# P^T of the second and third token group: 32x32 block transposes on VectorE and a way through DRAM in place of TensorE transposes

## The chip, the cores and the metric

The kernel runs on one core of one Trainium2 chip. The core has five engines that run side by side and wait for each other by semaphores: PE (TensorE, the matrix engine; PEld is its loading of weights), DVE (VectorE), ACT (ScalarE), POOL (GpSimd) and SP (SyncE, which here issues DMA transfers). The time is that of one execution in microseconds, the median of several runs; less is better.

## The reference, cut to what matters

Attention over a sliding window of 64 keys, and on its output a dense mixture of four experts with weights from `domain_probs`. The sizes are B = 4, H = 8, S = 576, D = 64; N = 2304 tokens, DM = 512, E = 4, F = 1024.

```python
scores = (1 / sqrt(D)) * (q @ k.T)                 # per batch and head
rel = pos[:, None] - pos[None, :]
scores = where((rel >= 0) & (rel < 64), scores, -1e9)
attn = exp(scores - scores.max(-1)); attn = attn / (attn.sum(-1) + 1e-9)
x = (attn @ v)  as (N, H * D)                      # P V
p = domain_probs / (domain_probs.sum(-1) + 1e-9)
for e in range(4):
    out += p[:, e] * (relu(x @ w1[e]) @ w2[e])
```

## The kernel before, in words

The 2304 tokens are cut into three token groups of 768 (`NGRP`, index n), and the attention into 36 groups of 64 queries (index g, twelve per token group: g 0 to 11, 12 to 23, 24 to 35). For one attention group, four pairs of heads are worked on together, so a tile has 128 partitions (two heads of 64 queries) and 4 x 128 columns (four pairs, 128 keys; only 64 keys where a batch begins). The steps of a group, with the names that the planner gives them, are:

- S (L302): scores on PE into a PSUM bank `sb`.
- m (L332, L336): DVE scales, masks and takes the row maximum; e (L343): ACT takes the exponentials, in `sm`; r (L352, L353): DVE takes the reciprocals of the sums; n (L360): POOL multiplies, which gives the normalised P in `sm`.
- T (L367): PE transposes P, four times 128 x 128, into a PSUM bank `tb`; t (L374): ACT or DVE copies it to `pt` in SBUF.
- V (L388): for two groups at a time, PE multiplies P^T with the values `vn` into `vb`; x (L398): ACT or DVE copies the result into `xr`, which is x transposed, for the token group.

The expert layer takes one unit of 256 hidden features at a time, 16 units per token group, 48 in all (index i). Seven products of a Strassen-like scheme, P1 to P7 (L623, 384 columns, six matmuls each, float32r as two parts "high" and "low"), give the hidden values of unit i in the banks X, Y and V; G steps (L707, y, 512 columns) multiply them with w2. The first two units of the first token group are done directly (d, L676). Between the products DVE forms sums from the banks (u2, u3, c22, c21, c12, all L642); the product P7 may only start when u2 has been read out of bank Y, P4 when u3 has, P3 when c22 has. ACT and DVE then make the two parts of the hidden values (hh L549, hl L552), which the G steps wait for. The weights come by DMA into `w1r` and `w2r`; POOL forms four combinations of w1 (L485), and ACT and DVE split them (L498, L502). When a token group is full, its quarters are combined and split by L423, L428 and L438 (tiles B and T).

The order is not written out by hand. A `Planner` holds every step with a cost per engine, a due time, the steps that it follows and the buffers that it takes; `order()` deals them out to the engines, and each engine then runs its instructions strictly in that order. PE's products and G steps have a fixed sequence among themselves (`seq`); the attention of the next token group is put between them. SP's transfers are steps too, and a transfer that waits for a buffer holds up those behind it on SP.

The change touches `Step.__init__` (L32), `admit` (L58) and the cost of SP steps (L105) in the planner, the list of buffers (L156), `make` (L192), and the steps T, t and V of a group (L364 to L393).

Of the kernel before, what the change touches and what calls it, by code (L numbers as in the profile page):

```python
# [8 lines left out]
F32 = mybir.dt.float32  # L9
# [11 lines left out]
LATENCY = dict(PE=0.25, ACT=0.12, DVE=0.12, POOL=0.15, SP=1.0)  # L21
# [9 lines left out]
class Step:  # L31
    def __init__(self, plan, name, engines, emit, due, after=(), takes=(), uses=(), seq=None, port=()):  # L32
        self.name, self.engines, self.emit, self.due, self.seq, self.port = name, engines, emit, due, seq, port
        self.after, self.takes, self.uses = [a for a in after if a is not None], list(takes), list(uses)
        self.done = None
        self.next = []
        for b in {*self.takes, *self.uses}:
            b.left += 1
        self.waits = len(self.after)
        for a in self.after:  # L40
            a.next.append(self)
        plan.steps.append(self)


class Planner:
# [5 lines left out]
    def order(self):  # L51
        clock = dict.fromkeys(("PE", "ACT", "DVE", "POOL", "SP"), 0.0)
# [3 lines left out]
        out = []  # L56

        def admit(s):  # L58
            slack = 0.6 if "PE" in s.engines and s.seq is None else 0.0
            s.ready = max((a.done + LATENCY[a.engine] for a in s.after), default=-slack) + slack  # L60
            for e in s.engines:
                ready[e].append(s)

# [4 lines left out]
        while left:  # L68
# [22 lines left out]
            t, e, s = best  # L91
# [11 lines left out]
            if e in s.port:  # L103
                port_free = end
            if e == "SP":  # L105
                clock[e] = t + 0.5
                dma_free = end = max(dma_free, t + 1.5) + s.engines[e]
            s.start, s.done, s.engine = t, end, e
            if s.seq is not None:
# [19 lines left out]
def kernel(ctx: ExitStack, tc: tile.TileContext, q, k, v, dprobs, w1, w2, out):  # L129
    nc = tc.nc  # L130
# [22 lines left out]

    slots = {}
    for kind, n in dict(
        qb=3, kt=2, vn=4, sm=3, pt=3, st=4, xr=1, w1r=2, w1a=1, w1b=1, w1c=1, w1d=1, w2r=1, w2s=3, h0=6, h1=8,  # L156
        s1=1, u2=1, u3=1, c22=1, c21=1, c12=1, acc=TPB * 2, B11=1, B21=1, B22=1, T1=1, T2=1, T3=1, T4=1,
    ).items():
        slots[kind] = [f"{kind}_{i}" for i in range(n)]
# [17 lines left out]
    dps = pool.tile([P, N // P, 1], F32, tag="dps", name="dps")  # L177

    SHAPES = dict(
        qb=([P, NP, P], F32), kt=([P, NP, W + P], F32), vn=([P, DM], F32), sm=([P, NP, P], F32), pt=([P, NP, P], F32), st=([P, 4, NP], F32),  # L180
        xr=([P, KC, G], F32), w1r=([P, 7, A], F32), w1a=([P, 2, 2, A], F32R), w1b=([P, 2, 2, A], F32R),
        w1c=([P, 2, 2, A], F32R), w1d=([P, 2, 1, A], F32R), w2r=([P, 2, DM], F32), w2s=([P, 2, 2, DM], F32R),
        h0=([P, 2, T], F32R), h1=([P, 2, T], F32R), acc=([P, DM], F32),
# [28 lines left out]
    def add(name, engines, emit, due, after=(), takes=(), uses=(), seq=None, port=()):  # L212
        return Step(plan, name, engines, emit, due, after, takes, uses, seq, port)
# [43 lines left out]
    for g in range(NG):  # L257
# [7 lines left out]
        nk = nkeys(g)  # L265
        u, o = divmod(g, 2)
        qb, vn, sm, pt, st = Buf("qb" + z), Buf("vn" + z), Buf("sm"), Buf("pt"), Buf("st")
        sb, tb = Buf("pa" + z), Buf("pa" + z)
        both = n > 0 or j >= GPB
        if j % 2 == 0 or not both:  # L270
            vb, pairs = Buf("pa" + z), []
# [92 lines left out]
        def transp(on, g=g, nk=nk, sm=sm, tb=tb):  # L364
            t = make(tb, f"tb{g}")
            for p in range(NP):
                nc.tensor.transpose(t[:nk, p * P : (p + 1) * P], sm.tile[:, p, :nk], ident)  # L367

        tr = add(f"T{g}", dict(PE=0.45), transp, due + 3, [nm], [tb], [sm])
        t_step[g] = tr  # L370

        def evac_t(on, g=g, nk=nk, tb=tb, pt=pt):
            t = make(pt, f"pt{g}").rearrange("s p j -> s (p j)")
            (nc.vector.tensor_copy if on == "DVE" else nc.scalar.copy)(t[:nk], tb.tile[:nk])  # L374

        ev = add(f"t{g}", dict(ACT=0.6, DVE=0.69), evac_t, due + 3.2, [tr], [pt], [tb])

        pairs.append((g, nk, vn, pt, ev, v_dma))
        if j % 2 == 0 and both:
            continue  # L380

        def pv(on, pairs=pairs, vb=vb):
            t = make(vb, f"vb{pairs[0][0]}").rearrange("s (p j) -> s p j", p=NP)
            for x, (_, nk, vn, pt, _, _) in enumerate(pairs):
                for p in range(NP):
                    for i in range(2):
# [446 lines left out]
```

## Time and profile before

| | us |
|---|---|
| median of 3 runs | 843.77 |
| lowest and highest run | 843.57, 844.07 |
| the profiled execution in all | 844.59 |
| span of the profile | 842.8 |
| PE busy | 834.9 (99%) |
| DVE busy | 549.9 (65%) |
| ACT busy | 357.3 (42%) |
| POOL busy | 324.1 (38%) |

The span runs from the first to the last instruction of the program; the execution has a little around it. Busy time of PE overlaps from one matmul to the next, since matmuls are pipelined: what a step costs in PE's queue is seen from the start of one group of matmuls to the start of the next. The granted TensorE clock is full in every slice of the page. In 40 equal slices PE stands at 8 or 9 tenths after the first, and DVE is fullest in the first slices and around 290 us. DMA engines are busy for more than half of a slice only in the first three.

### The profile page before, as it was taken

The page shows a single profiled execution, that of the slowest core. Times are in us where ns is not written, and L with a number is a line of the kernel's source. Part 1 is how long each engine was busy: PE and PEld are TensorE (multiplying, and loading weights), DVE is VectorE, ACT ScalarE, POOL GpSimd, SP SyncE. Part 2 cuts the span into 40 slices and gives each one's busy share as a digit, 9 for nine tenths or more (in the row PEclk, how much of TensorE's full clock was granted, in tenths as well). Part 3 has the DMA queues.
Part 4 walks back from the last instruction along what each step waited for, and adds up shares of the span by engine and source line. Part 5 has one row for each costly group of instructions (what it writes and reads, how often), then busy time and mean ns, then how long its engine had stood idle before and what let it go on. Part 6 is the DMA issues. An engine that isn't in the chain of part 4 may idle for free.

```text
span 842.8 us, 12925 instructions
## 1 busy us (share of the span) xinstructions
PE 834.9 (99%) x4814; PEld 749.5 (89%) x4814; DVE 549.9 (65%) x962; ACT 357.3 (42%) x819; POOL 324.1 (38%) x334
## 2 busy tenths in 40 slices
PE   8999999999999999999999999999999999999998
PEld 7998988888998888898998888889898889889887
DVE  5878755566665896466665766589556556566553
ACT  5756433344444363344443544335334333333320
POOL 4733633424334154443334433326334434434400
PEclk9999999999999999999999999999999999999999
DMA  9953212233233143232333202113312212112102
GB/s 334 288 163 119 90 55 100 75 94 113 81 114 101 63 145 117 84 107 63 121 98 107 88 26 91 61 50 111 115 51 79 71 51 90 61 51 97 31 24 75
DMA packets 45471, 81.23 MB, mean 96 GB/s; under 512 B 6368, under 2 KB 15840, under 8 KB 45408
## 3 DMA queue, kind: packets, MB, share of 16 engines
q1 hardware_dynamic: 44880, 80.14, 28.8%
q8 instruction: 38, 0.62, 0.3%
q10 hardware_dynamic: 528, 0.26, 0.1%
q14 instruction: 25, 0.20, 0.1%
HBM read 75.67 MB, written 4.72 MB: 95 GB/s over the span
## 4 chain that ended last, share of the span: by engine, by line
PE 98%; DVE 1%; DMA 1%; issue 0%; POOL 0%; ACT 0%; DVEq 0%; POOLq 0%
PE y L707 47%; PE Y L623 17%; PE V L623 11%; PE X L623 11%; PE sb L302 4%; PE vb L388 2%; PE d L676 2%; PE tb L367 2%; DMA kt<-in_k_dram 1%; PE yl L576 0%; PE sb L300 0%; DVE sm L332 0%; POOL sm L360 0%; DVE B L428 0%; DVE st L336 0%
## 5 line engine op out<-in xcount | busy, mean ns | idle before, releaser
L707 PE MATMUL y<-w2s,h 128*128 128x512 f32 x1716 | 444.0, 395 | 0.0
L707 PEld LDWEIGHTS y<-w2s,h 128*128 128x128 f32 x1716 | 316.6, 188 | 51.6
L485 POOL TENSOR_TENSOR w1r<-w1r 128x256 f32<-128x256 f32 x184 | 149.7, 819 | 192.7 <-DMA w1r<-in_moe_w_dram 141.0
L524 POOL TENSOR_TENSOR w2s<-w2r,w2s 128x512 fp32r<-128x512 f32 x96 | 132.2, 1389 | 227.6 <-ACT w2s L518 227.5
L642 DVE TENSOR_TENSOR u<-Y,s 128x384 f32<-128x384 f32 x92 | 51.1, 556 | 140.5 <-PE Y L623 140.5
L726 DVE SCALAR_TENSOR_TENSOR acc<-y,dp,acc 128x512 f32<-128x512 f32 x125 | 93.3, 747 | 23.4 <-PE y L707 23.4
L552 DVE SCALAR_TENSOR_TENSOR h<-c,h 128x384 fp32r<-128x384 f32 x138 | 83.6, 609 | 13.5 <-ACT h L549 13.2
L498 ACT CAST w1b<-w1r 128x512 fp32r<-128x512 f32 x46 | 28.5, 620 | 138.8 <-PE Y L623 138.3
L549 ACT ACTIVATE h<-c 128x384 fp32r<-128x384 f32 x138 | 72.3, 525 | 21.2 <-DVE c L642 20.3
L360 POOL TENSOR_TENSOR sm<-sm,st 128x512 f32<-128x512 f32 (+1 forms) x36 | 37.4, 1039 | 78.3 <-DVE st L353 55.7
L518 ACT CAST w2s<-w2r 128x1024 fp32r<-128x1024 f32 x48 | 50.4, 1051 | 25.3 <-PE y L707 21.6
L498 ACT CAST w1a<-w1r 128x512 fp32r<-128x512 f32 x48 | 29.8, 621 | 72.1 <-PE Y L623 68.0
L623 PE MATMUL Y<-T,w1c 128*128 128x384 f32 x276 | 55.8, 337 | 0.8 <-DVE u L642 0.8
L623 PE MATMUL V<-B,w1d 128*128 128x384 f32 x276 | 56.6, 340 | 0.0
L623 PE MATMUL Y<-T,w1b 128*128 128x384 f32 x276 | 56.6, 339 | 0.0
L623 PE MATMUL Y<-T,w1a 128*128 128x384 f32 x276 | 55.9, 337 | 0.0
L623 PE MATMUL X<-B,w1c 128*128 128x384 f32 x276 | 55.8, 336 | 0.0
L623 PE MATMUL X<-B,w1a 128*128 128x384 f32 x276 | 55.7, 336 | 0.0
L623 PE MATMUL V<-T,w1b 128*128 128x384 f32 x276 | 55.5, 335 | 0.0
L343 ACT ACTIVATE sm<-sm,st 128x128 f32<-128x128 f32 (+1 forms) x120 | 46.1, 386 | 21.7 <-DVE st L336 21.0
L623 PEld LDWEIGHTS Y<-T,w1c 128*128 128x128 f32 x276 | 49.3, 188 | 5.4 <-DVE u L642 1.5
L642 DVE TENSOR_TENSOR c<-Y,s 128x384 f32<-128x384 f32 x46 | 25.6, 557 | 43.1 <-PE Y L623 43.1
(79 smaller groups left out, 1016.9 us busy)
## 6 DMA issues: line engine op xcount, KB each, us to landing
w1r<-in_moe_w_dram SPq DMA_DIRECT2D x96, 256.0 KB, 3.5
w2r<-in_moe_w_dram SPq DMA_DIRECT2D x48, 512.0 KB, 3.5
qb<-in_q_dram SPq DMA_DIRECT2D x36, 256.0 KB, 3.8
vn<-in_v_dram SPq DMA_DIRECT2D x32, 256.0 KB, 4.1
kt<-in_k_dram SPq DMA_DIRECT2D x17, 384.0 KB, 5.0
out_dram<-acc SPq DMA_DIRECT2D x17, 256.0 KB, 2.0
vn<-in_v_dram SPq DMA_DIRECT2D x4, 128.0 KB, 4.1
kt<-in_k_dram ACTq DMA_DIRECT2D x1, 256.0 KB, 4.9
```

The costliest lines, as they stand in the source:

```text
L343: nc.scalar.activation(t[:, p, :nk], t[:, p, :nk], AF.Exp, bias=st.tile[:, 1, p : p + 1], accum_out=st.tile[:, 2, p : p + 1],)
L360: nc.gpsimd.tensor_tensor(out=t, in0=t, in1=rl.to_broadcast([P, NP, nk]), op=ALU.mult)
L485: nc.gpsimd.tensor_tensor(out=t[:, dst], in0=t[:, x], in1=t[:, y], op=op)
L498: f(t[:, 0], raw.tile[:, lo_:hi_])
L518: nc.scalar.copy(make(b, f"w2s{i}")[:, 0], raw.tile)
L524: nc.gpsimd.tensor_tensor(out=b.tile[:, 1, f], in0=raw.tile[:, f], in1=b.tile[:, 0, f].bitcast(F32), op=ALU.subtract)
L549: nc.scalar.activation(make(b, f"h{i}_{f}{t_}")[:, 0], src.tile[:, :T], AF.Relu)
L552: nc.vector.scalar_tensor_tensor(out=b.tile[:, 1], in0=src.tile[:, :T], scalar=0.0, in1=b.tile[:, 0].bitcast(F32), op0=ALU.max, op1=ALU.su ...
L623: nc.tensor.matmul(t[:, :T], wb.tile[:, a, wi, ws], cb.tile[:, x, c, :], start=first and m == 0, stop=m == 5, skip_group_check=True,)
L642: return lambda t, p_: nc.vector.tensor_tensor(out=t, in0=p_, in1=o.tile, op=ALU.add)
L707: nc.tensor.matmul(o, hh[:, a, ts], w[:, b, f, :], start=x == 0 and m == 0, stop=x == 1 and m == 5)
L726: nc.vector.scalar_tensor_tensor(out=ab.tile, in0=yb.tile, scalar=pc, in1=ab.tile, op0=ALU.mult, op1=ALU.add)
```

## The change

For the first token group (n = 0) all stays as it was. For the other two, P is no longer transposed on PE. DVE transposes it in blocks of 32 x 32 from `sm` into a tile `tp` (one buffer): in it each block stands where its 32 queries were, and inside it queries and keys are exchanged. SP then stores `tp` by four transfers, one for each 32 partitions, into a DRAM tile `hop` (two buffers), such that the blocks come to lie in the order of the keys, and one load brings `hop` into `pt`. The PSUM bank `tb` and its evacuation fall away for these groups. `pt` now holds, for each key, the four blocks of 32 queries outside and the head pairs inside, so P V reads a head's 64 queries as two runs of 32 columns.

In the planner, a step of P V gets 6 us of slack after its inputs in place of 0.6, the four stores count as four issues, and an issue of SP counts 0.45 in place of 0.5. One buffer of `vn` is given up for `tp`. Numbers below in names are the planner's buffers or running numbers.

```diff
@@ planner
-        self.done = None
+        self.done, self.issues, self.slack = None, 1, 0.6 if "PE" in engines and seq is None else 0.0
...
-            slack = 0.6 if "PE" in s.engines and s.seq is None else 0.0
-            s.ready = max((a.done + LATENCY[a.engine] for a in s.after), default=-slack) + slack
+            s.ready = max((a.done + LATENCY[a.engine] for a in s.after), default=-s.slack) + s.slack
...
-                clock[e] = t + 0.5
+                clock[e] = t + 0.45 * s.issues
@@ buffers
-        qb=3, kt=2, vn=4, sm=3, pt=3, st=4, xr=1, w1r=2, ...
+        qb=3, kt=2, vn=3, sm=3, tp=1, pt=3, hop=2, st=4, xr=1, w1r=2, ...
...
+            b.tile = dram.tile([4, 32, 4, P], F32, tag=b.slot, name=name)
@@ attention group
-        sb, tb = Buf("pa" + z), Buf("pa" + z)
+        sb, tb = Buf("pa" + z), Buf("tp" if n else "pa0")
...
+        else:
+            def transp(on, g=g, nk=nk, sm=sm, tb=tb):
+                t = make(tb, f"tp{g}")
+                blocks = sm.tile[:, :, :nk].rearrange("s p (b j) -> s b p j", j=32)
+                nc.vector.transpose(out=t[:, : nk // 32], in_=blocks)
+
+            t_step[g] = tr = add(f"T{g}", dict(DVE=0.69), transp, due + 3, [nm], [tb], [sm], port=("DVE",))
+
+            hop = Buf("hop")
+
+            def leave(on, g=g, nk=nk, tb=tb, hop=hop):
+                t = make(hop, f"hop{g}")
+                for a in range(4):
+                    nc.sync.dma_start(
+                        t[: nk // 32, :, a].rearrange("b j x -> j b x"),
+                        tb.tile[32 * a : 32 * (a + 1), : nk // 32].rearrange("j b p i -> j b (p i)"),
+                    )
+
+            def place(on, g=g, nk=nk, hop=hop, pt=pt):
+                nc.sync.dma_start(
+                    make(pt, f"pt{g}")[:nk].rearrange("k p j -> k (p j)"),
+                    hop.tile[: nk // 32].rearrange("b j a x -> (b j) (a x)"),
+                )
+
+            ev = add(f"t{g}", dict(SP=2.0), leave, due + 3.2, [tr], [hop], [tb])
+            ev.issues = 4
+            ev = add(f"u{g}", dict(SP=1.5), place, due + 3.4, [ev], [pt], [hop])
...
+                        if n == 0:
+                            pt_head = pt.tile[:nk, p, lo:hi]
+                        else:
+                            pt_head = pt.tile.rearrange("k p j -> k (p j)").rearrange("k (a p i) -> k a p i", a=4, p=NP)
+                            pt_head = pt_head[:nk, 2 * i : 2 * i + 2, p]
...
+        if n:
+            vv.slack = 6.0
```

**Place 1, P V of groups 32 and 33 on PE, and the transfers on SP.** Before, PE transposes group 33 (`tb`) and multiplies the pair (`vb`) two expert products later:

```order
L623 MATMUL V_5280<-B_1_3213,w1d_5237 128x384 x6
L367 MATMUL tb_5384<-ident,sm_5325 128x128 x4
L623 MATMUL X_5393<-B_1_3063,w1a_5273 128x384 x6
L707 MATMUL y_3_5409<-w2s_4942,h_01_5068 128x512 x3
L707 MATMUL y_3_5409<-w2s_4942,h_11_5017 128x512 x3
L388 MATMUL vb_5419<-pt_5227,vn_4759 64x64 x8
L388 MATMUL vb_5419<-pt_5400,vn_4761 64x64 x8
```

Now the pair stands behind the last y step (y_5) of the same two units, where before it stood within y_3:

```order
L662 MATMUL Y_5125<-T_1_3335,w1c_5076 128x384 x6
L746 MATMUL y_5_5203<-w2s_4880,h_01_4948 128x512 x3
L746 MATMUL y_5_5203<-w2s_4880,h_11_4870 128x512 x3
L424 MATMUL vb_5245<-pt_4964,vn_4582 64x64 x8
L424 MATMUL vb_5245<-pt_5143,vn_4928 64x64 x8
L662 MATMUL V_5145<-B_1_3289,w1d_5104 128x384 x6
```

Between the product in front of the old transpose and the new place of P V lie thirteen expert products, seven P and six G. On SP the four stores of group 33 (`hop`, printed as one row) and the load into `pt` now stand among the weight loads; a w1 load is between them:

```order
L552 DMA w2r_5034<-in_moe_w_dram 128x1024
L394 DMA hop_5099<-tp_5089 32x4x128 x4
L514 DMA w1r_5121<-in_moe_w_dram 128x512
L515 DMA w1r_5121<-in_moe_w_dram 128x512
L400 DMA pt_5143<-hop_5099 128x512
```

SP had only loads of weights, q, k and v and the stores of the result before; the row of `pt` is one that waits for transfers in front of it.

**Place 2, the start on PE.** This is unit 2, the first that is done by the seven products: Y is the bank of P6, P7 and P4, then V that of P3. Before:

```order
L623 MATMUL Y_1042<-T_0_913,w1a_892 128x384 x6
L302 MATMUL sb_1051<-kt_745,qb_738 128x128 x4
L623 MATMUL Y_1042<-T_0_883,w1b_932 128x384 x6
L367 MATMUL tb_1077<-ident,sm_990 128x128 x4
L302 MATMUL sb_1087<-kt_745,qb_847 128x128 x4
L623 MATMUL Y_1042<-T_0_935,w1c_904 128x384 x6
L623 MATMUL V_982<-B_0_819,w1d_687 128x384 x6
```

Now:

```order
L662 MATMUL Y_1010<-T_0_908,w1a_883 128x384 x6
L304 MATMUL sb_1020<-kt_749,qb_742 128x128 x4
L662 MATMUL Y_1010<-T_0_886,w1b_927 128x384 x6
L662 MATMUL Y_1010<-T_0_966,w1c_905 128x384 x6
L662 MATMUL V_957<-B_0_826,w1d_689 128x384 x6
```

The transpose of group 14 is gone, and the scores of group 17 have moved behind, so P7, P4 and P3 follow each other directly. On DVE the second u of this unit now stands ahead of two weight splits (w1a, w1b), behind which the sum c comes; before, both splits stood ahead of that u.

**Place 3, DVE at the end of unit 15**, where the third token group takes over. The y product that is second in PE's queue for the next unit pair waits for `h_10`. Before:

```order
L642 TENSOR_TENSOR c_15_3188<-Y_3108,s_15_3068 128x384
L726 SCALAR_TENSOR_TENSOR acc_5_1209<-y_5_3146,dp,acc_5_1209 128x512
L642 TENSOR_TENSOR c_15_3204<-V_3071,u_15_3125 128x384
L332 SCALAR_TENSOR_TENSOR sm_3216<-sb_3127,mask 128x512
L336 TENSOR_REDUCE st_3215<-sm_3216 128x4
L502 TENSOR_TENSOR w1c_3176<-w1r_2907,w1c_3176 128x512
L552 SCALAR_TENSOR_TENSOR h_11_3179<-c_15_3168,h_11_3179 128x384
L502 TENSOR_TENSOR w1d_3199<-w1r_2907,w1d_3199 128x256
L552 SCALAR_TENSOR_TENSOR h_10_3201<-c_15_3188,h_10_3201 128x384
```

Now, from the row after that first c (`c_15_3245`) on:

```order
L541 TENSOR_TENSOR w1b_3192<-w1r_2936,w1b_3192 128x512
L541 TENSOR_TENSOR w1c_3242<-w1r_2936,w1c_3242 128x512
L591 SCALAR_TENSOR_TENSOR h_11_3240<-c_15_3227,h_11_3240 128x384
L765 SCALAR_TENSOR_TENSOR acc_5_1182<-y_5_3185,dp,acc_5_1182 128x512
L467 TENSOR_TENSOR T_1_3215<-xr_1191,T_1_3215 128x768
L681 TENSOR_TENSOR c_15_3291<-V_3113,u_15_3173 128x384
L334 SCALAR_TENSOR_TENSOR sm_3297<-sb_3207,mask 128x512
L338 TENSOR_REDUCE st_3296<-sm_3297 128x4
L334 SCALAR_TENSOR_TENSOR sm_3315<-sb_3284,mask 128x4x64
L338 TENSOR_REDUCE st_3314<-sm_3315 128x4
L541 TENSOR_TENSOR w1d_3276<-w1r_2936,w1d_3276 128x256
L591 SCALAR_TENSOR_TENSOR h_10_3279<-c_15_3245,h_10_3279 128x384
```

Two pairs of score reductions stand ahead of `h_10` in place of one (the second of 64 keys), and w1b and a split of T have come into this stretch. On PE two score steps (25 and 26) have moved from just ahead of that y product to a place before the product whose sum is this first c, and the score step of 27 stands where they were.

## Rows read from the trace of the kernel before

**Rows 1.** the page, busy time of each engine: us (share of the span) xinstructions

```profile
PE 834.9 (99%) x4814; PEld 749.5 (89%) x4814; DVE 549.9 (65%) x962; ACT 357.3 (42%) x819; POOL 324.1 (38%) x334
```

**Rows 2.** timeline of PE, 136 us: start us, us, engine, line, operation, operands

```profile
135.92 0.60 PE L367 MATMUL tb<-ident,sm 128*128 128x128 f32 x4
136.28 1.32 PE L623 MATMUL X<-B,w1c 128*128 128x384 f32 x6
137.43 1.56 PE L707 MATMUL y<-w2s,h 128*128 128x512 f32 x6
138.83 1.20 PE L623 MATMUL Y<-T,w1c 128*128 128x384 f32 x6
139.87 1.55 PE L707 MATMUL y<-w2s,h 128*128 128x512 f32 x6
```

**Rows 3.** stretch, length, busy of PE, PEld, DVE, ACT, POOL; clock, DMA, GB/s

```profile
90.00:282.00 192.00, 192.00 (x1125) 172.47 (x1125) 122.34 (x209) 81.86 (x178) 76.39 (x79) 1.00 0.28 90
282.00:314.00 32.00, 32.00 (x169) 28.39 (x168) 30.88 (x48) 17.52 (x46) 11.66 (x12) 1.00 0.37 120
```

**Rows 4.** timeline of PE near 78 us

```profile
77.11 0.60 PE L367 MATMUL tb<-ident,sm 128*128 128x128 f32 x4
77.54 1.06 PE L302 MATMUL sb<-kt,qb 128*128 128x128 f32 x8
79.44 1.32 PE L623 MATMUL Y<-T,w1c 128*128 128x384 f32 x6 [0.84 <-DVE u L642]
```

**Rows 5.** groups by line, DVE: busy us, mean ns, idle before, releaser

```profile
L374 DVE COPY pt<-tb 128x512 f32<-128x512 f32 (+1 forms) x10 | 6.8, 684 | 1.3 <-PE tb L367 1.3
...
L423 DVE CAST T<-xr 128x768 fp32r<-128x768 f32 x3 | 1.7, 556 | 0.2
```

**Rows 6.** timeline of DVE near 78 us

```profile
78.23 0.68 DVE L502 TENSOR_TENSOR w1b<-w1r,w1b 128x512 fp32r<-128x512 f32 x1
78.83 0.55 DVE L642 TENSOR_TENSOR u<-Y,s 128x384 f32<-128x384 f32 x1
```

**Rows 7.** timeline of DVE near 300 us

```profile
295.96 1.79 DVE L502 TENSOR_TENSOR w1b<-w1r,w1b 128x512 fp32r<-128x512 f32 x1
297.67 0.54 DVE L642 TENSOR_TENSOR c<-Y,s 128x384 f32<-128x384 f32 x1
...
299.26 0.67 DVE L332 SCALAR_TENSOR_TENSOR sm<-sb,mask 128x512 f32<-128x512 f32 x1
...
300.57 1.23 DVE L502 TENSOR_TENSOR w1c<-w1r,w1c 128x512 fp32r<-128x512 f32 x1
...
302.52 1.01 DVE L552 SCALAR_TENSOR_TENSOR h<-c,h 128x384 fp32r<-128x384 f32 x2
```

**Rows 8.** timeline of PE near 300 us

```profile
295.52 1.55 PE L707 MATMUL y<-w2s,h 128*128 128x512 f32 x6
...
301.42 1.95 PE L302 MATMUL sb<-kt,qb 128*128 128x128 f32 x16
303.13 1.63 PE L707 MATMUL y<-w2s,h 128*128 128x512 f32 x6
```

**Rows 9.** DMA issues: count, KB each, median us from issue to landing

```profile
qb<-in_q_dram SPq DMA_DIRECT2D x36, 256.0 KB, 3.8
...
kt<-in_k_dram SPq DMA_DIRECT2D x17, 384.0 KB, 5.0
out_dram<-acc SPq DMA_DIRECT2D x17, 256.0 KB, 2.0
```

**Rows 10.** timeline of SP, the issue of a w1 load

```profile
195.01 0.33 SPq L475 DMA_DIRECT2D w1r<-in_moe_w_dram  x1
```

**Rows 11.** timeline of POOL, its first combinations of that load

```profile
200.37 1.89 POOL L485 TENSOR_TENSOR w1r<-w1r 128x256 f32<-128x256 f32 x2 [0.81 <-DMA w1r<-in_moe_w_dram]
```

**Rows 12.** timeline of ACT, the split of w1a from them

```profile
215.94 0.62 ACT L498 CAST w1a<-w1r 128x512 fp32r<-128x512 f32 x1 [2.03 <-PE Y L623]
```

**Rows 13.** timeline of PE, P V of a pair

```profile
489.79 1.15 PE L388 MATMUL vb<-pt,vn 128*64 128x64 f32 x32
```

More of the change, by code (lines that the diff above doesn't have):

```diff
@@ L155 @@
     for kind, n in dict(
-        qb=3, kt=2, vn=4, sm=3, pt=3, st=4, xr=1, w1r=2, w1a=1, w1b=1, w1c=1, w1d=1, w2r=1, w2s=3, h0=6, h1=8,
+        qb=3, kt=2, vn=3, sm=3, tp=1, pt=3, hop=2, st=4, xr=1, w1r=2, w1a=1, w1b=1, w1c=1, w1d=1, w2r=1, w2s=3, h0=6, h1=8,
         s1=1, u2=1, u3=1, c22=1, c21=1, c12=1, acc=TPB * 2, B11=1, B21=1, B22=1, T1=1, T2=1, T3=1, T4=1,
@@ L168 @@
     pool = ctx.enter_context(tc.tile_pool(name="pool", bufs=1))
+    dram = ctx.enter_context(tc.tile_pool(name="dram", bufs=1, space=bass.MemoryType.DRAM))
     psum = ctx.enter_context(tc.tile_pool(name="psum", bufs=1, space=bass.MemoryType.PSUM))
@@ L179 @@
     SHAPES = dict(
-        qb=([P, NP, P], F32), kt=([P, NP, W + P], F32), vn=([P, DM], F32), sm=([P, NP, P], F32), pt=([P, NP, P], F32), st=([P, 4, NP], F32),
+        qb=([P, NP, P], F32), kt=([P, NP, W + P], F32), vn=([P, DM], F32), sm=([P, NP, P], F32), pt=([P, NP, P], F32), tp=([P, 4, NP, 32], F32), st=([P, 4, NP], F32),
         xr=([P, KC, G], F32), w1r=([P, 7, A], F32), w1a=([P, 2, 2, A], F32R), w1b=([P, 2, 2, A], F32R),
@@ L194, in make @@
             b.tile = psum.tile([P, DM], F32, tag=b.slot, name=name)
+        elif b.kind == "hop":
+            b.tile = dram.tile([4, 32, 4, P], F32, tag=b.slot, name=name)
         else:
@@ L362 @@
         nm = add(f"n{g}", dict(POOL=0.05 + 0.00203 * NP * nk), norm, due + 2, [r], [], [sm, st], port=("POOL",))
[L364 to L374, printed above, removed]
@@ L376, with evac_t, transp @@
-        ev = add(f"t{g}", dict(ACT=0.6, DVE=0.69), evac_t, due + 3.2, [tr], [pt], [tb])
+        if n == 0:
+            def transp(on, g=g, nk=nk, sm=sm, tb=tb):
+                t = make(tb, f"tb{g}")
+                for p in range(NP):
+                    nc.tensor.transpose(t[:nk, p * P : (p + 1) * P], sm.tile[:, p, :nk], ident)
+            tr = add(f"T{g}", dict(PE=0.45), transp, due + 3, [nm], [tb], [sm])
+            t_step[g] = tr
+            def evac_t(on, g=g, nk=nk, tb=tb, pt=pt):
+                t = make(pt, f"pt{g}").rearrange("s p j -> s (p j)")
+                (nc.vector.tensor_copy if on == "DVE" else nc.scalar.copy)(t[:nk], tb.tile[:nk])
+            ev = add(f"t{g}", dict(ACT=0.6, DVE=0.69), evac_t, due + 3.2, [tr], [pt], [tb])
+        else:
+            def transp(on, g=g, nk=nk, sm=sm, tb=tb):
+                t = make(tb, f"tp{g}")
[18 more added lines that the diff above has]
+            ev = add(f"u{g}", dict(SP=1.5), place, due + 3.4, [ev], [pt], [hop])
@@ L380, with pv @@
             continue
-        def pv(on, pairs=pairs, vb=vb):
+        def pv(on, pairs=pairs, vb=vb, n=n):
             t = make(vb, f"vb{pairs[0][0]}").rearrange("s (p j) -> s p j", p=NP)
@@ L387, in pv @@
                         lo, hi = i * D, (i + 1) * D
+                        if n == 0:
+                            pt_head = pt.tile[:nk, p, lo:hi]
+                        else:
+                            pt_head = pt.tile.rearrange("k p j -> k (p j)").rearrange("k (a p i) -> k a p i", a=4, p=NP)
+                            pt_head = pt_head[:nk, 2 * i : 2 * i + 2, p]
                         nc.tensor.matmul(
                             t[lo:hi, p, x * W : (x + 1) * W], vn.tile[:nk, p * P + lo : p * P + hi],
-                            pt.tile[:nk, p, lo:hi], start=True, stop=True,
+                            pt_head, start=True, stop=True,
                         )
         vv = add(f"V{g}", dict(PE=0.2 + 0.47 * len(pairs)), pv, due + 4, [y for z_ in pairs for y in z_[4:]], [vb], [y for z_ in pairs for y in z_[2:4]])
+        if n:
+            vv.slack = 6.0
         def evac_x(on, n=n, lo=(j + 1 - len(pairs)) * W, hi=(j + 1) * W, vb=vb):
```

## The prediction

> **What bounds the kernel now.** I read the table of engines first. TensorE (PE) is busy for 834.9 of 842.8 us, VectorE (DVE) for 549.9, ScalarE (ACT) for 357.3, GpSimd (POOL) for 324.1 [rows 1]. The chain of waits says the same from the end backwards: PE's lines fill nearly all of it. The timeline of PE, third, shows the products of the expert layer start to start without a pause [rows 2]. So a microsecond taken from PE's queue is a microsecond of the kernel, unless PE then waits; one added elsewhere is free until PE waits for it. Where that could happen is read from the stretches, fourth: between 90 and 282 us DVE is busy 122.3 of 192.0 us, but 30.9 of 32.0 us between 282 and 314, where the second token group takes over [rows 3]. The other place where PE waits for DVE is at the start, 0.84 us at 79.44 [rows 4]. The change adds DVE work at both.
>
> **What leaves PE.** 24 steps of four transposes (groups 12 to 35) leave. Bars overlap, so I count starts. The transposes start at 135.92 and the next product at 136.28: 0.36 us. That product, the first after float32 work, takes until 137.43, 1.15 us, where the same kind takes 1.04 (138.83 to 139.87) [rows 2]. So a step costs 0.36 + 0.11 = 0.47 us among products. The three that touch another float32 step (12, 13, 14) cost 0.43 (77.11 to 77.54 [rows 4]). 21 x 0.47 + 3 x 0.43 = 11.2; since the starts are rounded to 0.01 us, I take **-11.0 us**. Their evacuations go too, nearly all from ACT, which was waiting for PE anyway: nothing for the sum.
>
> **What DVE gets.** 24 block transposes of 128 x 512. The trace has none. The cheapest pass over SBUF is a cast of 768 columns in 0.56 us, so 0.37 for 512; two passes of the evacuation's length would be 1.37. I take 0.69, the copy of just these elements, the nearest row [rows 5]. 24 x 0.69 = 16.6 us, against 69.7 idle us in the second stretch alone [rows 3], where it is hidden by DVE's waiting for PE. Each transpose waits for POOL's normalisation and holds up what is behind it on DVE; its place comes when that is due, as PE's did.
>
> The Trainium skill ("VectorE: DVE Perf Modes", sections The three transpose paths and Rules for kernel authors) speaks against such a move: TensorE for a 128x128 transpose where a PSUM destination is fine; its table gives VectorE 311 ns for one in bf16 and TensorE 390. As an estimate from that table a step would be 4 x 0.311 = 1.24 us on DVE, near the upper end above and so near the first rival below; its 390 ns is not what PE pays here, where four take 0.36 us.
>
> **The transition at 300 us.** The order puts two score reductions (the pairs of L332 and L336, in the changed file L334 and L338) ahead of the split h_10 that the second y product waits for. Before, DVE ran without a gap from the sum c at 297.67 to the two splits that start at 302.52, the first of which, 0.55 long, is the one: 5.40 us [rows 7]. Now the stretch has in addition w1b (0.60 start to start [rows 6]), a split of T of 768 columns (half as much again, 0.90) and a half-width reduction, an estimate of 0.9 between the half and the whole of the full pair's 1.31 (299.26 to 300.57): 7.8 us. PE covers it from the end of the product before c (295.52) to the y product (303.13): 7.61 us, of which two score steps take 1.71 [rows 8]. These two now stand earlier and one of 0.9 comes in: cover 6.8. So PE waits **+1.0 us**. Bounds: 0, if DVE starts c early, and 2.1, if w1b meets POOL again as in the 1.79 us that it took at 295.96 [rows 7].
>
> **The start.** In before P4 waits for u at 79.44, with transposes and a score step ahead of it since 77.11 [rows 4], and u at 78.83 stands behind two weight splits [rows 6]. Now transposes and score step leave that place and u goes ahead of the splits: it ends near 78.2, P4 starts at 78.25, and the next sum c behind the two splits lets P3 start near 79.9. Before, P3 started 1.15 after P4, at 80.6. That is 0.7 us earlier, with 0.43 + 0.9 us of PE work gone from between: 0.65 is not gained, **+0.7**. The first 60 us are dealt anew too, since loads and buffers differ. Between 0, where all goes as before, and twice the 0.84 that PE waits here, I take **+0.5**, for the shorter queue in which transposes and P V cover each other.
>
> **The way through DRAM.** For each group SP issues four stores of 64 KB and a load of 256 KB, and the load waits in SP's queue until the stores have landed. Stores land 2.0 us after issue, q loads of 256 KB 3.8, kt's 5.0 [rows 9]; an issue takes 0.33 [rows 10]. So 0.69 + 4 x 0.33 + 2.0 + 0.33 + 3.8 = 8.1 us from transpose to P^T; with 5.0 for both landings, issues twice as long and 1.37 for the transpose 14.7. P V stands later by enough: of pair 32/33, six y products of 1.40 and seven of 1.04 [rows 2] lie between the place of the old transpose and the new one of P V, 15.7 us. So PE does not wait: **0**. Behind the waiting load stand w1, w2, q, k and v loads, late by 2 to 4 us. A w1 load issued at 195.01 [rows 10] is first used by POOL at 200.37, two of its four combinations take 1.89 us [rows 11], and the cast of w1a at 215.94 waited not for them but for PE to leave the old buffer [rows 12]: 15.6 - 3.8 = 11.8 us are spare. One vn buffer less moves v loads, whose data P V now needs later.
>
> **P V itself** keeps its matmuls, but reads P^T as two runs of 32 columns instead of one of 64. A pair takes 1.15 us [rows 13]. The trace has no float32 operand in split runs. Bounds: 0 and, if split runs stream at half speed, 12 x 1.15 = 13.8 us. I take 0: its own row, with the same count of columns, is the nearest. Below nothing it can't go, for the columns stay.
>
> **Sum.** -11.0 + 1.0 + 0.7 + 0.5 = -8.8 us. The profiled execution took 844.59 us in all, so 835.8; the runs' median, 843.77, is 0.8 below it. I predict **835.0 us**.
>
> **Rivals.**
> *DVE becomes a bound at the pinch points.* If a transpose costs 1.37 us, each of those in the full stretches (three before 90 us, one near 290) adds 0.7, and w1b's long form another 1.1: 835.0 + 3.9 = 838.9. For it: DVE is 96% busy there [rows 3]. Against: most transposes fall where DVE waits for PE.
> *SP's queue turns the gain round (slower).* The load waits for four stores of 512-byte pieces, and everything behind it on SP waits too. Up to a hop of 15.7 us nothing is lost; beyond that each of 12 pairs loses the excess. From 16.5 us on (12 x 0.8 = 9.6) the kernel is slower than before; at 17 it loses 12 x 1.3 = 15.6, so 835.0 + 15.6 = 850.6. For it: SP works strictly in order, and stores of that shape are not in the trace. Against: twice the landing time of a store still fits.
> *Two runs of 32 stream slowly:* 835.0 + 13.8 = 848.8. It turns the sign from 8.8 / 12 = 0.73 us a pair.
> *Nothing waits:* 843.8 - 11.0 = 832.8, if PE's waits for DVE do not grow at all.
>
> **How the numbers follow.** The forecast (833.5 to 837) has 0.72; nothing waits 0.08; the DVE pinch 0.11; SP's queue 0.05; slow runs 0.04. A change under 0.2% (1.7 us) can't be told from none. Faster: 0.72 + 0.08 + 0.10 = 0.90; slower 0.07, the last two less their mild forms; same 0.03, those and the worst of the pinch. The range 832.3 to 840.0 holds the first three cases and leaves the last two out.
>
> **What would show it.** Right: no transposes on PE after 50 us and P V pairs still 1.15 us long; the block transpose near 0.69; a wait of PE for DVE of about 1 us at the second y product after the change of token group, and two smaller ones near 76 to 80 us; no wait of P V for the load of pt; SP waiting about 2 us before each such load. Wrong: P V waits for a DMA, P V's bar grows, or PE's idle time grows by more than 4 us.

## The result, and the profile after

The changed kernel takes 836.76 us (median of 6 runs, 836.09 to 837.53), the kernel before 843.85 beside it: a ratio of 0.9913 with a 95% interval of 0.9902 to 0.9924. Its profiled execution took 836.75 us in all, with a span of 834.8 where before had 842.8.

The page's busy times after, to set beside [rows 1]:

```profile
PE 824.6 (99%) x4717; PEld 740.0 (89%) x4718; DVE 559.8 (67%) x982; ACT 346.4 (41%) x798; POOL 324.8 (39%) x335
```

PE's 10.3 us less go with the 96 matmuls of the 24 transpose steps that left; it is still busy for 99%. DVE has 9.9 more.

Timeline of PE in the steady state after, the same steps as in [rows 2] and a P V as in [rows 13]:

```profile
133.14 1.21 PE L662 MATMUL Y<-T,w1b 128*128 128x384 f32 x6
134.19 1.55 PE L746 MATMUL y<-w2s,h 128*128 128x512 f32 x6
135.57 1.23 PE L662 MATMUL X<-B,w1c 128*128 128x384 f32 x6
```
```profile
497.12 1.15 PE L424 MATMUL vb<-pt,vn 128*64 128x64 f32 x32
```

Products and y products follow each other with nothing between (1.05 us from 133.14, 1.38 from 134.19), and P V of a pair is 1.15 us long as before: reading P^T in two runs of 32 costs nothing.

Groups by line (as [rows 5]), then the DMA issues (as [rows 9]), then what SP's queue waited for (us in total, times, longest us), all after:

```profile
L385 DVE STREAM_TRANSPOSE tp<-sm 128x512 f32<-128x512 f32 (+1 forms) x24 | 16.3, 679 | 0.2 <-POOL sm L362 0.2
```
```profile
hop<-tp SPq DMA_DIRECT2D x88, 64.0 KB, 1.8
pt<-hop SPq DMA_DIRECT2D x22, 256.0 KB, 3.7
```
```profile
SPq L400 <- DMA hop<-tp: 4.9, 6, 2.1
```

The block transpose takes 0.68 us on the mean. From its start to the landing of P^T the way through DRAM takes 9.2 us in the median (6.5 to 14.0 over the 24 groups), and the second load of a pair lands 7.1 us or more before PE reads it; no instruction of PE waits for it. SP waited for a landed store only six times. Its longer wait is ahead of the stores, for the transposes (100.0 us in all, 21 times). POOL's waits for w1 loads are 173.1 us in all where they were 141.0, and PE pays nothing for either.

Where PE does wait. At the start, timelines of PE and of DVE after (as [rows 4, 6]):

```profile
74.47 1.32 PE L662 MATMUL Y<-T,w1b 128*128 128x384 f32 x6
76.77 1.30 PE L662 MATMUL Y<-T,w1c 128*128 128x384 f32 x6 [0.98 <-ACT w1b L537]
78.35 1.33 PE L662 MATMUL V<-B,w1d 128*128 128x384 f32 x6 [0.27 <-DVE c L681]
79.52 1.20 PE L662 MATMUL X<-B,w1a 128*128 128x384 f32 x6
```
```profile
74.75 0.69 DVE L334 SCALAR_TENSOR_TENSOR sm<-sb,mask 128x512 f32<-128x512 f32 x1 [0.33 <-PE sb L304]
...
76.08 0.55 DVE L681 TENSOR_TENSOR u<-Y,s 128x384 f32<-128x384 f32 x1
```

P4 starts 2.30 us after P7, though a product has 1.15 at most: the sum u it needs, which DVE makes from P7's own result, ends at 76.63, behind the two score reductions of group 16, the first of them at 74.75. (The profile puts that wait down to ACT's cast of w1b, which ended at the same time; but this product reads w1c, and in experiment 11 it starts ahead of that cast's end.) The reductions are the smaller part: without them P4 still starts 2.05 after P7 (experiment 11), since the transposes and scores that PE had in this place before are gone. P3 then waits 0.27 for the sum c.

At the change of token group, PE, DVE and POOL after (as [rows 7, 8]):

```profile
296.83 1.55 PE L746 MATMUL y<-w2s,h 128*128 128x512 f32 x6
298.21 1.00 PE L304 MATMUL sb<-kt,qb 128*128 128x64 f32 x8
300.32 1.30 PE L662 MATMUL V<-T,w1b 128*128 128x384 f32 x6 [1.11 <-DVE c L681]
301.47 1.33 PE L746 MATMUL y<-w2s,h 128*128 128x512 f32 x5
303.14 0.50 PE L746 MATMUL y<-w2s,h 128*128 128x512 f32 x1 [0.34 <-DVE h L591]
```
```profile
295.98 2.21 DVE L591 SCALAR_TENSOR_TENSOR h<-c,h 128x384 fp32r<-128x384 f32 x1
...
299.63 0.54 DVE L681 TENSOR_TENSOR c<-V,u 128x384 f32<-128x384 f32 x1
300.10 0.68 DVE L334 SCALAR_TENSOR_TENSOR sm<-sb,mask 128x512 f32<-128x512 f32 x1
...
301.42 0.41 DVE L334 SCALAR_TENSOR_TENSOR sm<-sb,mask 128x256 f32<-128x256 f32 x1
...
302.53 1.02 DVE L591 SCALAR_TENSOR_TENSOR h<-c,h 128x384 fp32r<-128x384 f32 x2
```
```profile
295.47 2.29 POOL L477 TENSOR_TENSOR xr<-xr 128x768 f32<-128x768 f32 x1
```

There are two waits, not one. The product V at 300.32 waits 1.11 us for the sum c that ends at 300.17, and the last matmul of the y product at 303.14 waits for the split h, which has the reductions of groups 26 and 27 (300.10, 301.42) ahead of it. Against the usual spacing of such steps they cost 1.30 and 0.62 us, 1.9 together. The split h at 295.98 took 2.21 us, where one takes 0.55: it started while POOL worked from 295.47 on, and ended 0.43 after that instruction of POOL. The Trainium skill ("SBUF — State Buffer", section SBUF: two separate sides) says that a VectorE operation with two SBUF inputs and a GpSimd operation that reads SBUF exclude each other for a whole instruction; these rows agree with it.

### The profile page after: what moved, and what is told of

The parts are those of the page before. It is cut to its first block, busy times and chain, and to the rows that moved or that the text cites. A ratio compares the mean times of both kernels' runs of the same rounds, so it can differ in the third digit from the quotient of the medians.

```text
span 834.8 us, 12896 instructions
## 1 busy us (share of the span) xinstructions
PE 824.6 (99%) x4717; PEld 740.0 (89%) x4718; DVE 559.8 (67%) x982; ACT 346.4 (41%) x798; POOL 324.8 (39%) x335
## 4 chain that ended last, share of the span: by engine, by line
PE 95%; DVE 3%; DMA 1%; POOL 0%; issue 0%; ACT 0%; POOLq 0%
PE y L746 47%; PE Y L662 17%; PE X L662 12%; PE V L662 11%; PE sb L304 4%; PE vb L424 2%; PE d L715 2%; DMA qb<-in_q_dram 1%; PE tb L371 1%; DMA kt<-in_k_dram 1%; PE yl L615 0%; DVE h L591 0%; DVE st L338 0%; DVE sm L334 0%; POOL sm L362 0%
## 5 line engine op out<-in xcount | busy, mean ns | idle before, releaser
L524 POOL TENSOR_TENSOR w1r<-w1r 128x256 f32<-128x256 f32 x184 | 147.0, 805 | 194.4 <-DMA w1r<-in_moe_w_dram 173.1
L681 DVE TENSOR_TENSOR c<-V,u 128x384 f32<-128x384 f32 x92 | 50.9, 553 | 6.6 <-PE V L662 5.1
L662 PEld LDWEIGHTS V<-T,w1b 128*128 128x128 f32 x276 | 49.3, 188 | 5.2 <-issue 1.2
```

Of the source, the lines that this page charges most:

```text
L524: nc.gpsimd.tensor_tensor(out=t[:, dst], in0=t[:, x], in1=t[:, y], op=op)
L662: nc.tensor.matmul(t[:, :T], wb.tile[:, a, wi, ws], cb.tile[:, x, c, :], start=first and m == 0, stop=m == 5, skip_group_check=True,)
L681: return lambda t, p_: nc.vector.tensor_tensor(out=t, in0=p_, in1=o.tile, op=ALU.add)
```

## The experiments

**1. The planner's part alone.** Every group transposes on PE; three vn buffers and the SP price stay.

```diff
-                clock[e] = t + 0.5
+                clock[e] = t + 0.45 * s.issues
-        qb=3, kt=2, vn=4, sm=3, pt=3, st=4, xr=1, w1r=2, w1a=1, w1b=1, w1c=1, w1d=1, w2r=1, w2s=3, h0=6, h1=8,
+        qb=3, kt=2, vn=3, sm=3, tp=1, pt=3, hop=2, st=4, xr=1, w1r=2, w1a=1, w1b=1, w1c=1, w1d=1, w2r=1, w2s=3, h0=6, h1=8,
```

> No group is transposed on VectorE and none goes through DRAM; what stays of the change is the planner's price for SP (0.45 us a DMA issue in place of 0.5) and three vn buffers in place of four. Theory A (the gain is the PE time of the 24 transposes, 0.43 to 0.47 us each, less new waits of PE at the start and at the change of token group): 843.8 us, no change within 0.4. Rival R (the new order of loads gives or costs something by itself): 1 us or more away from 843.8, and in the first 60 us the scores of group 10 again wait for a q load as in the changed kernel.

845.15 us, ratio 1.0015 (1.0007 to 1.0024): slower, so theory A was wrong here. Rival R had the size, but not its sign: no score step of PE waits for a q load in its trace. The median lies 1.6 us above that of the kernel before beside it (843.51) and 1.3 above the 843.85 of the result, the profiled execution only 0.7 above before's, which was itself 0.7 above its median. The steps of its profile stand 0.7 us later than before's from 50 us to the end, with this at 42 us, in a timeline of PE:

```profile
42.01 0.60 PE L372 MATMUL tb<-ident,sm 128*64 128x128 f32 x4
42.87 0.66 PE L372 MATMUL tb<-ident,sm 128*128 128x128 f32 x4 [0.27 <-POOL sm L363]
```

Before, the transposes of groups 9 and 10 stand apart, at 39.37 and 44.57, with other work between; here they follow each other, and the second waits for POOL. The loss of the first 60 us is there without any work added to DVE. From the start of the first to the start of the second it is 0.86 us, where such a step costs 0.43 [rows 4]; the rest is spread.

**2. and 3. Half of the groups each.**

```diff
+        hops = n == 2          # experiment 3: n == 1
-        sb, tb = Buf("pa" + z), Buf("tp" if n else "pa0")
+        sb, tb = Buf("pa" + z), Buf("tp" if hops else "pa" + z)
...
-        if n == 0:
+        if not hops:
...
-        if n:
+        if hops:
             vv.slack = 6.0
```

> Only the 12 groups of the third token group (24 to 35) use the block transpose and DRAM; 0 to 23 transpose on PE. The order around 300 us is then that of the kernel before (one score step ahead of the last product of the first token group, two after the second product of the next). Theory A: 12 x 0.47 = 5.6 us less and no new wait, so 843.8 - 5.6 = 838.2 us. Rival W (each group pays a small wait for DRAM or for SP's queue, which makes the 3 us between the 11.0 saved and the 8.0 seen): half of the gain, 840.2 us.

> Only the 12 groups of the second token group (12 to 23) use the block transpose and DRAM. Theory A: 9 x 0.47 + 3 x 0.43 = 5.5 us less, but all of the start's loss (1.2 us) and, since the scores of groups 25 to 27 still crowd around 300 us, 1 to 1.9 us of wait there: 843.8 - 5.5 + 1.2 + 1.5 = 841.0 us. Rival W: 840.2 us, as much as with groups 24 to 35 alone.

Groups 24 to 35: 840.13 us, ratio 0.9952 (0.9940 to 0.9965). Groups 12 to 23: 841.62, ratio 0.9978 (0.9969 to 0.9986). The first is 1.9 us above theory A's number and on W's; but both carry the loss of experiment 1, and against its 845.15 they gain 5.0 and 3.5, not the same. What a group brings is read from the trace, between the same two products (first of units 17 and 29) before and in experiment 2:

```profile
315.87 1.20 PE L623 MATMUL X<-B,w1a 128*128 128x384 f32 x6
```
```profile
523.86 1.29 PE L623 MATMUL X<-B,w1a 128*128 128x384 f32 x6
```
```profile
316.75 1.20 PE L663 MATMUL X<-B,w1a 128*128 128x384 f32 x6
```
```profile
519.27 1.20 PE L663 MATMUL X<-B,w1a 128*128 128x384 f32 x6
```

207.99 us before and 202.52 now: 5.47 less for 12 groups, 0.456 each. Both stretches hold the same number of matmuls for scores (72), P V (160) and y (432); before has 48 transposes more. W has no place: nothing waits between. In experiment 3 PE waits at 75 us (0.98 and 0.30) and at 300 us (1.29 and 0.41) as in the whole change (0.98 and 0.27, 1.11 and 0.34).

**4. Scores later.** Three score steps are held back behind products.

```diff
+    named = {s.name: s for s in plan.steps}
+    for late, first in {'S25': 'G7_01', 'S26': 'P7_16', 'S27': 'P4_16'}.items():
+        named[late].after.append(named[first])
+        named[first].next.append(named[late])
+        named[late].waits += 1
     steps = plan.order()
```

> The changed kernel, with the score steps of groups 25, 26 and 27 held back in the planner until the second y product, P7 and P4 of the unit at 300 us have gone, so that their reductions no longer stand on VectorE ahead of the sum c and the split h that PE waits for there. Theory A: the 1.9 us that PE waits at 298 to 303 us go, and the scores stand later among products at the same price: 836.8 - 1.9 = 834.9 us. Rival D (VectorE is late there for the split of T and for splits stretched beside GpSimd, not for the scores): no change, 836.8 us, with PE's waits still there.

835.04 us, ratio 0.9902 (0.9887 to 0.9917), which does not part it from the whole change. Its span, 832.8, is 2.0 shorter, but 1.3 of that stands already at 51 us, in an order that is the same in both, so it is a difference between executions. At 300 us only 0.7 is gained; of the timeline of PE there:

```profile
296.34 1.30 PE L662 MATMUL V<-T,w1b 128*128 128x384 f32 x6 [0.52 <-DVE c L681]
```

PE waits less for c (0.52), but it waits. Theory A had the right engine and a third of the cause.

**5. The old price of an issue.**

```diff
-                clock[e] = t + 0.45 * s.issues
+                clock[e] = t + 0.5 * s.issues
```

> The changed kernel with the planner's price for a DMA issue at 0.5 us again, as before the change, instead of 0.45; nothing else differs. The planner-only kernel lost 0.7 us in its profile between 40 and 50 us, with a wait of 0.5 us of the transposes of group 10 for GpSimd's normalisation there. Theory P (that price alone deals the first 60 us anew, and so costs the 0.5 to 0.7): 836.8 - 0.6 = 836.2 us, with no wait at the transposes of group 10. Rival B (the three vn buffers, or loads that come anew, do it): 836.8 us, with that wait still there.

837.07 us, ratio 0.9912 (0.9899 to 0.9926), and the transposes of group 10 still wait. With it the changed kernel's first 60 us are in the same order. So theory P falls for the whole change: what else puts them in that order stays open.

**6. P V 22/23 earlier.**

```diff
-            vv.slack = 6.0
+            vv.slack = 0.6 if g == 23 else 6.0
```

> The changed kernel with P V of groups 22 and 23, the last of the second token group, placed some 4.6 us earlier (a slack of 0.6 for this pair instead of 6.0; its load had landed 8.5 us before it was read). Rival V (the splits that wait for this pair come too late at the change of token group, and that is the wait at 298 to 303 us): 836.8 - 1.9 = 834.9 us. Theory A2 (VectorE's own work from 282 to 303 us is the bound there, so work taken from PE in it gives nothing back): 836.8 us, waits of PE there as long or longer.

837.80 us, ratio 0.9925 (0.9913 to 0.9938), and in the timeline of PE:

```profile
300.95 1.28 PE L662 MATMUL V<-T,w1b 128*128 128x384 f32 x6 [1.97 <-DVE c L681]
```

The wait for c grew from 1.11 to 1.97, and unit 17 begins 0.8 us later, set against the steps ahead of this place. Rival V falls: P V was work that PE had while DVE caught up. Taking work from PE in this stretch gives nothing back.

**7. A lighter DVE at the change of token group.** Beside the edit of experiment 4 and the old issue price:

```diff
-    for late, first in {'S25': 'G7_01', 'S26': 'P7_16', 'S27': 'P4_16'}.items():
+    for late, first in {'S25': 'G7_01', 'S26': 'P7_16', 'S27': 'P4_16', 'T24': 'G7_01'}.items():
-        x = add(f"x{g}", dict(ACT=act(NP * W * len(pairs)), DVE=dve(NP * W * len(pairs))), evac_x, due + 4.2, [vv], [xr[n]], [vb])
+        x = add(f"x{g}", dict(ACT=act(NP * W * len(pairs))) if g == 23 else dict(ACT=act(NP * W * len(pairs)), DVE=dve(NP * W * len(pairs))), evac_x, due + 4.2, [vv], [xr[n]], [vb])
```

> The changed kernel with three edits: the issue price 0.5; the scores of groups 25 to 27 held back behind the second y product, P7 and P4 of the unit at 300 us, and the block transpose of group 24 behind that y product too; the evacuation of P V 22/23 on ScalarE alone. That takes from VectorE between 282 and 303 us 0.69 for the transpose, 0.69 for the evacuation and 3.5 for three pairs of score reductions. Theory A2: the waits of 1.9 us there go or fall under 0.7 (0.68 of them went with the scores alone), and 0.6 us come from the start: 836.8 - 1.5 - 0.6 = 834.7 us, or 833.9 if all go. Rival D (splits stretched beside GpSimd hold VectorE): waits of 1.2 us stay as with the scores alone, 835.5 us.

834.61 us, ratio 0.9886 (0.9873 to 0.9900), better than the whole change with intervals that do not touch; only experiment 11 has a lower median, by 0.05. Its timeline of PE at that place:

```profile
295.06 1.55 PE L746 MATMUL y<-w2s,h 128*128 128x512 f32 x6
296.45 1.21 PE L662 MATMUL V<-T,w1b 128*128 128x384 f32 x6
```

No wait is left there; the steps from unit 22 on stand 1.9 us earlier than in the changed kernel. The start has gained nothing, as in experiment 5. Splits stretched beside POOL are still there (w1b took 1.79 us), so D falls too: they cost PE only where DVE has too much besides. How much of the last 1.2 us is the evacuation's and how much the transpose's was not parted.

**8. Each transpose twice.**

```diff
-            nc.vector.transpose(out=t[:, : nk // 32], in_=blocks)
+            for _ in range(2):
+                nc.vector.transpose(out=t[:, : nk // 32], in_=blocks)
```

> The changed kernel with each block transpose on VectorE made twice into the same tile: 24 x 0.69 = 16.6 us more for VectorE, in the same order. Theory A2 (a transpose costs PE only where VectorE is the bound, at the start and from 282 to 303 us): 0.7 us for that of group 24 and 0 to 0.7 for each of groups 13 and 14, so 836.8 + 1.4 = 838.2 us (837.5 to 838.9). Rival F (VectorE has room everywhere): 836.8 us. Rival G (each transpose stands in PE's path): 836.8 + 16.6 = 853.4 us.

836.32 us, ratio 0.9906 (0.9893 to 0.9920): no change, with 24 transposes more (DVE is busy for 576.7 us, not 559.8). Timeline of DVE around the transpose of group 24, in the changed kernel and here:

```profile
282.19 0.70 DVE L385 STREAM_TRANSPOSE tp<-sm 128x512 f32<-128x512 f32 x1
283.40 0.75 DVE L765 SCALAR_TENSOR_TENSOR acc<-y,dp,acc 128x512 f32<-128x512 f32 x1 [0.51 <-PE y L746]
```
```profile
281.69 1.45 DVE L386 STREAM_TRANSPOSE tp<-sm 128x512 f32<-128x512 f32 x2
283.06 0.71 DVE L766 SCALAR_TENSOR_TENSOR acc<-y,dp,acc 128x512 f32<-128x512 f32 x1
```

After the one transpose DVE was idle for 0.51 us; the second fills that. So even this one costs nothing: my A2 was wrong on it, F right. Of the 24 transposes of the changed kernel 19 have such a gap of DVE, most of them a wait for PE, ahead of one of the next four instructions; the other five cost nothing either; what hides them was not looked at.

**9. and 10. A longer way through DRAM.**

```diff
-                nc.sync.dma_start(
-                    make(pt, f"pt{g}")[:nk].rearrange("k p j -> k (p j)"),
-                    hop.tile[: nk // 32].rearrange("b j a x -> (b j) (a x)"),
-                )
+                t = make(pt, f"pt{g}")[:nk].rearrange("k p j -> k (p j)")
+                for _ in range(2):          # experiment 10: range(4)
+                    nc.sync.dma_start(t, hop.tile[: nk // 32].rearrange("b j a x -> (b j) (a x)"))
```

> The changed kernel with each load of P^T from DRAM issued twice into the same tile, the second behind the landing of the first: one more landing, 3.7 us, in each way through DRAM, and as much longer in SP's queue. In the changed kernel the second load of a pair lands 7.1 to 13.2 us (one 26.8) before PE reads it. Theory H (the way through DRAM is hidden with 7 us to spare): 836.8 us, no wait of P V for a load. Rival Q (SP's queue is near its limit, so the loads of weights behind it come late): a microsecond or more slower, with PE, ACT or GpSimd waiting for w1, w2 or q loads.

> The changed kernel with each load of P^T issued four times into the same tile, each behind the one before: three landings more, about 3 x 3.8 = 11.4 us. Theory H: seven pairs had 7.1 to 9.0 us to spare, 59.5 together, and one 10.5, so PE waits 7 x 11.4 - 59.5 = 20.3, and 0.9 for the one: 836.8 + 21 = 858 us, with P V waiting 2 to 4 us for pt in those pairs. Rival (more room than it looks, since PE's wait gives the next way through DRAM more time): under 845 us. Rival Q: over 870 us, with waits for weights added.

Twice: 835.68 us, ratio 0.9905 (0.9890 to 0.9920), no change. The way through DRAM was 12.0 us in the median, and at least 4.6 were to spare. Four times: 862.98 us, ratio 1.0223 (1.0185 to 1.0261), with a way of 17.8 us in the median. Theory H had the size, but not the place. What PE waited for in it:

```profile
PE X L661 <- DVE h L590: 6.7, 1, 6.7
...
PE y L745 <- DVE acc L764: 2.6, 1, 2.6
PE vb L423 <- DMA pt<-hop: 2.2, 2, 1.9
```

P V waited only 2.2 us for P^T. The row that is left out is a wait of 3.6 us for POOL's split of w2. The longest wait followed back, by rows of SP, ACT, DVE and PE:

```profile
135.87 8.32 SPq L402 DMA_DIRECT2D pt<-hop  x4
144.29 0.69 SPq L551 DMA_DIRECT2D w2r<-in_moe_w_dram  x1
```
```profile
148.87 1.04 ACT L556 CAST w2s<-w2r 128x1024 fp32r<-128x1024 f32 x1 [12.46 <-DMA w2r<-in_moe_w_dram]
149.82 0.61 ACT L536 CAST w1b<-w1r 128x512 fp32r<-128x512 f32 x1
```
```profile
150.47 1.35 DVE L540 TENSOR_TENSOR w1b<-w1r,w1b 128x512 fp32r<-128x512 f32 x1 [8.79 <-ACT w1b L536]
```
```profile
154.56 2.29 PE L661 MATMUL X<-B,w1a 128*128 128x384 f32 x6 [6.74 <-DVE h L590]
156.64 2.76 PE L745 MATMUL y<-w2s,h 128*128 128x512 f32 x6
159.20 1.34 PE L661 MATMUL Y<-T,w1a 128*128 128x384 f32 x6
```

The four loads hold SP for 8.32 us; the w2 load behind them goes out at 144.29, ACT splits it at 148.87 and w1b only after that; DVE, which works in order, waits 8.79 us for w1b, the split h stands behind it, and PE waits 6.74 for h. So the order of two queues carries one late load to a product that does not use it. The wait for POOL is of the same kind: POOL stood 19.0 us for a w1 load that SP had issued behind four such loads, and its split of w2 came behind that. The wait for acc came by another way, the one buffer `tp`; DVE:

```profile
123.55 0.71 DVE L385 STREAM_TRANSPOSE tp<-sm 128x512 f32<-128x512 f32 x1 [7.19 <-DMA hop<-tp]
```

The stores that empty `tp` stand behind four loads on SP, the next transpose waits 7.19 us for them, and the accumulation that frees the bank of a y product stands behind it on DVE. This is rival Q's way in the main, with the size of H; Q had named only late loads. Together PE waited 15.2 us at these four places (2.95, 6.74, 3.56 and 1.93 in order of time). They cost more: set against the changed kernel, the steps fall back by 5.0, 9.3, 5.7 and 3.7 us there (first products of units 5 and 6, 6 and 8, 20 and 21, 25 and 26), 23.7 of the 26.9 us between the spans. What came on top of the waits is in the last section.

**11. Row maxima of group 16 later**, in the kernel of experiment 7.

```diff
-    for late, first in {'S25': 'G7_01', 'S26': 'P7_16', 'S27': 'P4_16', 'T24': 'G7_01'}.items():
+    for late, first in {'S25': 'G7_01', 'S26': 'P7_16', 'S27': 'P4_16', 'T24': 'G7_01', 'm16': 'c22_2'}.items():
```

> The kernel of the lighter VectorE stretch (issue price 0.5, scores 25 to 27 and transpose 24 held back, evacuation 22/23 on ScalarE) with one edit more: the score reductions of group 16, which stood 1.3 us on VectorE ahead of the sum u that P4 waits for at 75 us, come behind the sums u and c. Theory A2 (at the start too PE waits for what stands ahead on VectorE): of the waits of 1.26 at P4 and 0.53 at P3 in the first unit of products, 0.4 and 0.5 go, 834.6 - 0.9 = 833.7 us. Rival (the sums wait for PE's own product, not for the reductions): 834.6 us.

834.56 us, ratio 0.9890 (0.9874 to 0.9907), no gain over 834.61. Its timeline of PE at the start and 20 us on, and of DVE there:

```profile
76.37 1.28 PE L662 MATMUL Y<-T,w1c 128*128 128x384 f32 x6 [0.74 <-DVE u L681]
77.49 1.20 PE L662 MATMUL V<-B,w1d 128*128 128x384 f32 x6
```
```profile
97.90 0.50 PE L746 MATMUL y<-w2s,h 128*128 128x512 f32 x1 [0.94 <-DVE h L591]
```
```profile
75.67 0.56 DVE L681 TENSOR_TENSOR u<-Y,s 128x384 f32<-128x384 f32 x1 [1.12 <-PE Y L662]
...
92.36 0.69 DVE L334 SCALAR_TENSOR_TENSOR sm<-sb,mask 128x512 f32<-128x512 f32 x1 [0.34 <-PE sb L304]
...
94.29 1.65 DVE L591 SCALAR_TENSOR_TENSOR h<-c,h 128x384 fp32r<-128x384 f32 x1
```

The wait at P3 is gone. That at P4 is 0.74, where it was 0.99: the sum u now starts as soon as P7 has ended, at 75.67, and P4 2.05 us after P7 instead of 2.30. So at P4 the rival is right but for 0.25 us, and the wait that is left is for PE's own product. The reductions of group 16 now stand at 84.48. The new order also brings the next score step forward (91.27 on PE, 95.81 in experiment 7), so its reductions stand at 92.36, in a stretch that DVE also fills with long splits, and the y product waits 0.94 for h at 97.90. What was gained was given back later: the first product of unit 3 is 1.06 earlier than in experiment 7, that of unit 5 0.16 later.

## Why the prediction came out

*Transposes off PE, -11.0.* Right: 24 x 0.456 = 10.9 by experiment 2.

*The block transpose, 0.69, hidden.* Right: 0.68, and hidden with room for a second one (experiment 8). Why it costs what a copy costs was not looked into. The estimate of 1.24 us from the table of the Trainium skill ("VectorE: DVE Perf Modes", The three transpose paths) was too high; the measurement decides, 0.70 for one of 128x512. The rival of a DVE pinch by transposes was priced too high: a second transpose cost nothing in the full stretches either (experiment 8).

*The start, +0.7.* Right, and by the way forecast. From the start of P7 to the next unit's first product, before took 5.69 us (75.96 to 81.65 in its trace), now 5.05 (74.47 to 79.52), though 1.2 us of transposes and scores left it: 0.6 lost. The step put P4 2.29 us behind P7 and P3 1.65 behind P4 (78.25 and 79.9, with P7 at 75.96); it was 2.30 and 1.58. Its u at 78.2 already stood behind the two reductions; how much they hold up P4, 0.25 us, only experiment 11 showed.

*The first 60 us, +0.5.* Right in size (the direct products of the second half start at 56.89, before at 57.12: 0.23 gained where two transposes, 0.86, left, so 0.6 lost), but not known closely: by medians the planner's part alone cost 1.3 to 1.6 (experiment 1), and the start of these direct products varies from 55.57 to 57.35 among the kernels here that have the changed kernel's order up to there. The reason was wrong at least in part: the new order brought two transposes together (experiment 1), and a score step waited 0.26 for a q load; that the queue was too short was not shown.

*The change of token group, +1.0.* This term was mis-sized: 1.9. The step let DVE take the sum c on time and only the split h come late. But c itself began at 299.63, behind a split of 2.21 us, and PE waited twice, 1.30 and 0.62 beyond the usual spacing. The step's upper bound of 2.1 holds this; it had a split stretched beside POOL in it, though w1b and not h. The engine and the reductions were named rightly; that the whole stretch from 283 us is DVE's bound, in which PE's own work is free filling, came out only in experiments 4, 6 and 7.

*The way through DRAM, 0.* Right, with 9.2 us for 8.1. "SP waiting about 2 us before each such load" was wrong: other loads stand between stores and load, and 18 of the 24 loads did not wait for their stores. The warning of the rival that SP's queue decides from some 16 us on is borne out by experiment 10, through late weights and the one buffer `tp` rather than P V.

*P V, 0.* Right.

Together -10.9 + 0.6 + 0.6 + 1.9 = -7.8; the spans differ by 8.0. The medians differ by 7.1, since before's profiled execution lay 0.7 above its median and the changed one's on it. So the forecast of 835.0 was 1.8 low: 0.9 from the transition, the rest from carrying over the 0.8 by which before's profiled execution was slow. The measured time lies 0.2 inside the upper end of the forecast's 833.5 to 837.

## What to carry to other kernels

Work taken from the bounding engine is worth its start-to-start spacing, except in stretches where that engine waits for another: find these first, since there its own work is free and each microsecond of the other engine counts. A long detour through DRAM costs nothing while its slack lasts, and most of the price is then paid by what stands behind it in the issuing queue, by way of engines that work in order. A product that needs a sum of the product just ahead of it wants other work between the two. Moving a step out of one full stretch moves others with it, and helps only if what lands in the next stretch finds room there.

## What the runs showed of the hardware

After a pause of PE its clock fell. Stretches of experiment 10 (length, busy of PE, PEld, DVE, ACT, POOL; granted clock, DMA share, GB/s):

```profile
154.00:159.00 5.00, 4.45 (x12) 3.96 (x13) 4.46 (x9) 1.71 (x4) 2.42 (x3) 0.50 0.33 109
159.00:170.00 11.00, 11.00 (x76) 9.58 (x77) 5.31 (x9) 2.97 (x5) 3.27 (x4) 0.98 0.12 46
```

Behind the 6.7 us in which PE stood, the granted clock was 0.50, the level of 1.2 GHz, and the next two steps took 2.08 and 2.56 us from start to start (154.56, 156.64, 159.20) where 1.04 and 1.39 are usual: 2.2 us more than the wait itself. Behind the other three waits of experiment 10, of 2.65, 3.28 and 1.93 us, it fell too: a mean of 0.66 was granted from 125 to 130 us, 0.72 from 386 to 392, 0.57 from 487 to 491. At each of the four places the steps fell back by 1.8 to 2.5 us more than PE waited (experiment 10). Not every such wait is followed by a fall: behind the 1.97 us of experiment 6 the granted clock was 1.00 from 301 to 306 us. In the changed kernel, whose longest wait is 1.1 us, the mean granted clock is 1.0.
